# Pairs of chunks in the first expert matmul, state decay on GpSimd, and 64-column array tiles for PV and the state term, in a fused attention and MLP kernel

## The chip, the cores and the metric

The kernel runs on one core of one Trainium2 chip. The metric is device time in microseconds (us), the median of several executions. The time and the trace of a run are of the same single core. The calls ran on several chips, so runs of different calls are compared by their ratios to the kernel before, which ran beside them. All executions used here are in the undisturbed ("fast") state; the granted TensorE clock of the profiled ones is 0.996 to 1.000 of full.

## The reference

A chunked linear attention with decay feeds a two-layer MLP with an ELU between the layers. Cut to what matters:

```python
# B, H, S, D = 4, 8, 768, 64; x: 3072 tokens x 512; w_in 512 x 2048; w_out 2048 x 512
for b in range(nb):                       # blocks of 64 positions
    intra = einsum('bhic,bhjc->bhij', qb, kb) * Dmask
    intra = einsum('bhij,bhjd->bhid', intra, vb)            # "PV"
    inter = einsum('bhid,bhde->bhie', qb * lam_pow, kv_state)   # "state term"
    out[:, :, sl] = intra + inter
    kv_state = lam_block * kv_state + einsum('bhsd,bhse->bhde', kb * rev_pow, vb)
h = x @ w_in
g = where(h > 0, h, exp(min(h, 0)) - 1)
return g @ w_out
```

## The kernel before

The kernel works in chunks of 128 positions of one batch row: 24 chunks `g`, six per row. Each chunk goes through transposes of q and k (`T`, `psT`), scores (`S`, `psS`), a masked product (`E`, `pp`), PV with the state term (`P`, `psO`, copied to `xt`), and the state update (`U`, `psU`, `st`). The MLP takes `xt`: `mm1` makes 512 columns of h in one PSUM bank (`psH`), ScalarE (ACT) makes exp and relu of it, VectorE (DVE) combines them to `g`, and `mm2` accumulates the output in `psM`. TensorE (PE) runs a fixed list of these units. The opening is written out by hand (`OPEN`), the rest is generated from offsets (`AT`).

```python
GPE = 10                       # chunks below 10 are transposed on PE, the others by DMA
POOL_ORDER = "iota q1 k1 v1 v0 i1 i0 k2 q2 v2 o0 o1 i3 i2 ..."   # GpSimd: loads, k decay (d)
OPEN = "V0 Z1 z1 V1 ... T0 T1 S0 S1 P0 P1 1:0:0 T2 1:1:0 S2 2:0:0 ..."
# ... "1:g:j" is unit j of mm1 of chunk g, "2:g:j" of mm2
AT = {"W": -13, "T": -9, "S": -8, "P": -5, "U": -3}

def att_P(g):                                                  # PV and state term
    ...
    for hp in range(NHP):                                      # four pairs of heads
        for hh in range(2):
            b0 = 4 * hp + hh        # v stands beside zeros, so that 128 columns hold one head
            nc.tensor.matmul(po[:, hp, :], lhsT=vt[:, b0 : b0 + 2, :],          # L322
                rhs=Pt[(g, hh)][:, hp, :], start=(hh == 0), stop=(hh == 1 and cb == 0))
        if cb > 0:
            nc.tensor.matmul(po[:, hp, :], lhsT=st[b][cb % 2][:, hp, :],        # L327
                rhs=qt[:, hp, :], start=False, stop=True)
    ...

def att_U(g):                                                  # state update
    ...                                                        # four matmuls, psU
    for hh in range(2):
        ...
        (nc.gpsimd if g >= GPE else nc.vector).tensor_tensor(  # decay, L356
            out=tmp[r], in0=old[r, :, r], in1=upp[r]..., op=ALU.mult)
        nc.vector.tensor_tensor(out=new[r, :, r], in0=tmp[r], in1=pu[r, :, r], op=ALU.add)

def mm1(g, j):
    ...
    for f in range(FB):                                        # four blocks of 128 columns of h
        for kk in range(NHP):
            nc.tensor.matmul(pH[:, f, :], lhsT=wi16[i][:, kk, w * 128 : (w + 1) * 128],
                rhs=xt[g][:, kk, :], start=(kk == 0), stop=(kk == NHP - 1))     # L388
    nc.scalar.activation(e[:], pH[:], AF.Exp)
    nc.scalar.activation(pH[:], pH[:], AF.Relu)
```

## Time and profile before

| | before |
|---|---|
| time, median of 3 | 222.96 us (222.66 to 223.24) |
| span in the profile | 221.4 us |
| first matmul starts | 5.43 us |
| last matmul starts | 218.06 us |
| GpSimd busy | 88.6 us |
| VectorE busy | 138.6 us |

The lines of the page that the argument rests on stand in the prediction below. PE, DVE, ACT and POOL (GpSimd) are engines, PEld is weight loading on TensorE. A row of forty digits gives the busy tenths of forty equal slices. In the chain of work that ended last, each row is start, duration, engine, what was written and a count. A duration there runs until the next link takes over, so a stretch of PE links without a gap is PE's pace.

A busy PE is not a streaming PE, so I also took the start of every matmul from the trace and compared the distance to the next start with the distance seen in an undisturbed stream: 55.7 ns for 128 columns, 109 for 256, 215.7 for 512, and half of 55.7 where two tiles run at once. What is over is a **switch** where the two neighbours use different array tiles, and a **wait** otherwise (a switch over 0.3 us counts as 0.12 us of switch and the rest as wait). So PE's time from first to last start splits into stream, switches and waits. Before, these are 197.7 us, 3.0 us (26 switches) and 11.9 us. In the opening many matmuls of 128 columns start 107 ns apart, half the later rate, and this excess is counted under waits: some 2.9 us before, 2.5 after the change.

### The profile page before, as it was taken

How to read it: one execution, taken by the hardware profiler on the slowest of the kernel's cores; microseconds unless marked ns; L12 is line 12 of the kernel's file. 1: busy time of each engine (PE TensorE's matmuls, PEld its weight loads, DVE VectorE, ACT ScalarE, POOL GpSimd, SP SyncE). 2: the span in 40 equal slices, each digit the busy share in tenths (PEclk: the TensorE clock that was granted, in tenths of full speed). 3: DMA queues.
4: the chain of work that ended last, by engine and by line, in shares of the span. 5: the costliest groups of instructions: out<-in, count | busy, mean ns of one | idle time of the engine just before them, and what ended most of it. 6: DMA issues, size and time to landing. Idle time of an engine off the chain costs nothing.

```text
span 221.4 us, 6086 instructions
## 1 busy us (share of the span) xinstructions
PE 207.1 (94%) x2548; PEld 156.3 (71%) x2548; DVE 138.6 (63%) x238; ACT 134.8 (61%) x255; POOL 88.6 (40%) x102
## 2 busy tenths in 40 slices
PE   0598999999999999999999999999999999999993
PEld 0486677768768776787787787787787777777761
DVE  5744745489978978666666666656657646634330
ACT  5745657766768566636636636646646645656760
POOL 8996990829972809508508508122000000000000
PEclk9999999999999999999999999999999999999999
DMA  7999999999999999968998998803304401101102
GB/s 114 169 182 186 195 200 167 139 169 120 166 140 181 127 164 135 141 84 93 143 100 100 132 108 95 144 0 98 94 3 98 96 3 47 52 1 50 47 3 95
DMA packets 99804, 24.26 MB, mean 110 GB/s; under 512 B 90432, under 2 KB 96832, under 8 KB 99776
## 3 DMA queue, kind: packets, MB, share of 16 engines
q0 software_dynamic: 78720, 13.37, 83.8%
q1 hardware_dynamic: 20912, 10.49, 22.3%
q8 instruction: 20, 0.33, 0.6%
q14 instruction: 8, 0.07, 0.1%
q10 hardware_dynamic: 144, 0.00, 0.0%
HBM read 27.27 MB, written 6.29 MB: 152 GB/s over the span
## 4 chain that ended last, share of the span: by engine, by line
PE 79%; DVE 11%; ACT 5%; DMA 2%; issue 1%; SPq 0%; DVEq 0%; ACTq 0%
PE psH L388 34%; PE psM L409 33%; PE psO L322 5%; DVE g L376 3%; PE psS L300 3%; DVE stt L356 2%; DMA raw_k<-in_k_dram 2%; PE psO L327 2%; DVE pp L309 2%; PE psU L344 2%; DVE qT L288 1%; DVE st L360 1%; ACT e L393 1%; ACT psH L394 1%; PE psT L281 1%
## 5 line engine op out<-in xcount | busy, mean ns | idle before, releaser
L388 PEld LDWEIGHTS <-wi 128*128 128x128 f16 x1536 | 94.0, 98 | 22.0 <-issue 2.2
L388 PE MATMUL psH<-xt,wi 128*128 128x128 f16 x1536 | 102.2, 220 | 1.8 <-ACT xt L333 0.7
L393 ACT ACTIVATE e<-psH 128x512 f32<-128x512 f32 x96 | 57.3, 597 | 68.3 <-PE psH L388 68.0
L409 PE MATMUL psM<-wo,g 128*128 128x512 f16 (+1 forms) x388 | 97.6, 377 | 0.8 <-DVE osb L422 0.5
L376 DVE SCALAR_TENSOR_TENSOR g<-e,psH 128x512 f16<-128x512 f32 x96 | 65.6, 684 | 44.1 <-ACT psH L394 42.8
L394 ACT ACTIVATE psH<-psH 128x512 f32<-128x512 f32 x96 | 56.9, 593 | 0.0
L409 PEld LDWEIGHTS <-g 128*128 128x128 f16 x388 | 33.7, 98 | 26.8 <-issue 0.7
L309 DVE TENSOR_TENSOR pp<-psS,mask 128x512 f16<-128x512 f32 x48 | 30.7, 682 | 5.1 <-PE psS L300 5.1
L107 POOL DMA_DIRECT2D vz<-in_v_dram x14 | 15.1, 1085 | 38.5 <-PE psU L344 38.0
L169 POOL TENSOR_TENSOR kd<-kn,ks 128x512 f16<-128x512 f16 x20 | 21.3, 1073 | 11.2 <-DMA kn<-in_k_dram 10.6
L322 PE MATMUL psO<-pp,vz 128*128 128x128 f16 x192 | 19.1, 226 | 1.2 <-DVE pp L309 1.2
L360 DVE TENSOR_TENSOR st<-stt,psU 64x256 f16<-64x256 f32 x32 | 13.4, 419 | 7.3 <-PE psU L344 6.3
L335 DVE TENSOR_TENSOR xt<-psO,qs 128x512 f16<-128x512 f32 x14 | 9.7, 691 | 11.9 <-PE psO L327 11.9
L322 PEld LDWEIGHTS <-vz 128*128 128x128 f16 x192 | 15.1, 101 | 2.5 <-issue 1.8
L424 ACT COPY osb<-psM 128x512 f32<-128x512 f32 (+1 forms) x24 | 13.9, 579 | 4.5 <-PE psM L409 4.5
L356 POOL TENSOR_TENSOR stt<-st,upp 64x256 f32<-64x256 f16 x20 | 12.2, 608 | 10.3 <-DVE st L360 9.5
L107 POOL DMA_DIRECT2D qn<-in_q_dram x13 | 14.8, 1142 | 0.5 <-DMA wi<-in_moe_w_in_dram 0.3
L327 PE MATMUL psO<-qT,st 128*128 128x128 f16 x80 | 14.4, 219 | 0.0
L107 POOL DMA_DIRECT2D kn<-in_k_dram x13 | 14.4, 1107 | 0.0
L288 DVE TENSOR_TENSOR qT<-psT,qs 128x512 f16<-128x512 f16 x10 | 6.6, 681 | 5.2 <-PE psT L281 5.2
L281 PE MATMUL psT<-ident,qn 128*128 128x128 f16 x40 | 4.6, 247 | 5.4 <-DVE qn L122 5.4
L333 ACT CAST xt<-psO 128x512 f16<-128x512 f32 x10 | 5.9, 588 | 6.0 <-PE psO L322 4.0
(41 smaller groups left out, 90.2 us busy)
## 6 DMA issues: line engine op xcount, KB each, us to landing
out_dram<-osb SPq DMA_DIRECT2D x23, 256.0 KB, 3.4
qn<-in_q_dram POOLq DMA_DIRECT2D x10, 256.0 KB, 7.6
kn<-in_k_dram POOLq DMA_DIRECT2D x10, 256.0 KB, 7.4
vz<-in_v_dram POOLq DMA_DIRECT2D x10, 256.0 KB, 8.2
wi<-in_moe_w_in_dram POOLq DMA_DIRECT2D x8, 256.0 KB, 8.3
wo<-in_moe_w_out_dram POOLq DMA_DIRECT2D x8, 256.0 KB, 8.8
vz<-in_v_dram POOLq DMA_DIRECT2D x4, 128.0 KB, 5.9
qn<-in_q_dram POOLq DMA_DIRECT2D x3, 128.0 KB, 6.4
```

Source lines behind the costliest of these rows:

```text
L107: nc.gpsimd.dma_start(out=dst.rearrange("p b h d -> p (b h) d"), in_=src)
L169: nc.gpsimd.tensor_tensor(out=kd[:], in0=of(kg, g), in1=ks[:].unsqueeze(2).broadcast_to([128, H, 64]), op=ALU.mult,)
L309: nc.vector.tensor_tensor(out=P[:], in0=pts[hh][:], in1=mask[:, hh::2, :], op=ALU.mult)
L322: nc.tensor.matmul(po[:, hp, :], lhsT=vt[:, b0 : b0 + 2, :], rhs=Pt[(g, hh)][:, hp, :], start=(hh == 0), stop=(hh == 1 and cb == 0), skip_ ...
L327: nc.tensor.matmul(po[:, hp, :], lhsT=st[b][cb % 2][:, hp, :], rhs=qt[:, hp, :], start=False, stop=True, skip_group_check=True,)
L356: (nc.gpsimd if g >= GPE else nc.vector).tensor_tensor(out=tmp[r], in0=old[r, :, r], in1=upp[r].unsqueeze(2).broadcast_to([64, NHP, 64]), ...
L360: nc.vector.tensor_tensor(out=new[r, :, r], in0=tmp[r], in1=pu[r, :, r], op=ALU.add)
L376: nc.vector.scalar_tensor_tensor(out=g[:], in0=e[:], scalar=-1.0, in1=r[:], op0=ALU.add, op1=ALU.min)
L388: nc.tensor.matmul(pH[:, f, :], lhsT=wi16[i][:, kk, w * 128 : (w + 1) * 128], rhs=xt[g][:, kk, :], start=(kk == 0), stop=(kk == NHP - 1),)
L393: nc.scalar.activation(e[:], pH[:], AF.Exp)
L394: nc.scalar.activation(pH[:], pH[:], AF.Relu)
L409: nc.tensor.matmul(psM[g][:, cols], lhsT=gts[(g, j)][:, f, :], rhs=wo16[i][:, w, cols], start=first and f == 0, stop=end and f == FB - 1, ...
```

## The change

Four things are meant to take work off TensorE and VectorE:

- `mm1` takes two chunks at once from chunk 4 on: one weight load and 256 moving columns.
- PV and the state term stop multiplying by zeros: each head gets its own 64-column half of the array, and two heads run at the same time.
- The state decay goes to GpSimd for all chunks, as its own step (`att_M`) ahead of the update.
- Chunks 8 and 9 are transposed by DMA (`GPE = 8`), and order of loads and units is rearranged to suit, with seven units of mm2 held back for the end (`LAGU = 7`).

```diff
-    GPE = 10
+    GPE = 8
+    GSIZE = {**{g: 1 for g in range(4)}, **{g: 2 for g in range(4, NG, 2)}}
     POOL_ORDER = (
-        "iota q1 k1 v1 v0 i1 i0 k2 q2 v2 o0 o1 i3 i2 q3 i5 k3 o2 d0 o3 i4 v3 o5 o4 d2 o7 i6 d3 "
+        "k2 v1 q2 iota q1 k1 i1 v0 i0 o1 v2 i3 o0 i2 q3 o2 k3 d0 d2 i4 d1 i5 o3 o7 v3 o5 o4 d3 "
...
     OPEN = (
-        "V0 Z1 z1 V1 z0 v3:1 Z0 z3 z2 T0 T1 S0 S1 P0 P1 1:0:0 T2 1:1:0 S2 2:0:0 Z2 P2 1:2:0 "
+        "v3:1 Z2 Z0 z2 Z1 V0 z0 T0 z3 z1 V1 T1 S0 T2 S1 P0 S2 P1 1:0:0 P2 U0 1:1:0 1:2:0 2:0:0 "
...
-    LAGU, LAG_END = 3, 4
+    LAGU = 7
...
-    nc.scalar.dma_start(out=lam_b[:], in_=lam.unsqueeze(0).broadcast_to([128, H]))
+    nc.sync.dma_start(out=lam_b[:], in_=lam.unsqueeze(0).broadcast_to([128, H]))
...     # raw_q stays on the sync queue, behind lam_b; raw_k goes to ScalarE's queue
         for hp in range(NHP):
-            for hh in range(2):
-                b0 = 4 * hp + hh
+            for hh, r in enumerate(R):                  # R: partitions 0-63 and 64-127
                 nc.tensor.matmul(
-                    po[:, hp, :], lhsT=vt[:, b0 : b0 + 2, :], rhs=Pt[(g, hh)][:, hp, :],
+                    po[r, hp, :], lhsT=vt[:, 4 * hp + 2 * hh, :], rhs=Pt[(g, hh)][:, hp, :],
...
             if cb > 0:
-                nc.tensor.matmul(
-                    po[:, hp, :], lhsT=st[b][cb % 2][:, hp, :], rhs=qt[:, hp, :],
+                for r in R:
+                    nc.tensor.matmul(
+                        po[r, hp, :], lhsT=st[b][cb % 2][:, hp, r], rhs=qt[:, hp, :],
...
+    def att_M(g):                                       # the decay, always GpSimd
...
-        for f in range(FB):
-            i, w = wi_of[j * FB + f]
+        for f in range(FB // n):                        # n: 1 or 2 chunks
+            i, w = wi_of[j * (FB // n) + f]
             for kk in range(NHP):
                 nc.tensor.matmul(
-                    pH[:, f, :], lhsT=wi16[i][:, kk, w * 128 : (w + 1) * 128],
-                    rhs=xt[g][:, kk, :], start=(kk == 0), stop=(kk == NHP - 1),
+                    pH[:, f * n * 128 : (f + 1) * n * 128],
+                    lhsT=wi16[i][:, kk, w * 128 : (w + 1) * 128],
+                    rhs=xg[g0][:, kk, :], start=(kk == 0), stop=(kk == NHP - 1),
                 )
```

In the changed kernel's trace the lines are: mm1 L428 (was L388), mm2 L450 (L409), PV L332 (L322), state term L338 (L327), scores L310 (L300), update L382 (L344), decay L365 (L356), `st` L393 (L360), `g` L411 (L376), transposes L291 (L281).

## The prediction

> **What bounds the kernel now.** I read the page's busy shares and 40 slices first, then the chain that ended last in order of time, then the waits of 20 to 90 us.
>
> ```profile
> PE 207.1 (94%) x2548; PEld 156.3 (71%) x2548; DVE 138.6 (63%) x238; ACT 134.8 (61%) x255; POOL 88.6 (40%) x102
> ...
> PE   0598999999999999999999999999999999999993
> ...
> DMA  7999999999999999968998998803304401101102
> ```
>
> TensorE (PE) is busy in every slice but the ends, at the full clock. The DMA engines are full until about 95 us, VectorE (DVE) never. Busy does not mean streaming, so I take the pace from the chain:
>
> ```profile
> 102.98 0.45 PE psH L388 x8
> 103.43 0.55 PE psS L300 x16
> 103.98 0.97 PE psM L409 x4
> 104.95 0.89 PE psH L388 x16
> 105.84 0.86 PE psM L409 x4
> ...
> 109.36 0.11 PE psO L322 x2
> 109.47 0.06 PE psO L327
> ```
>
> Sixteen mm1 matmuls of 128 columns take 0.89 us, 56 ns each; four mm2 matmuls of 512 columns take 0.86 us, 216 ns each. PV and the state term (psO) also go at 56 ns. Nothing lies between them: in this stretch PE runs at its streaming rate, so mm1's many weight loads are hidden already. Multiplying out the page's counts: mm1 1536 x 55.7 ns = 85.6 us; mm2 380 x 216 plus 8 of 256 columns x 109 = 82.8; PV 192 x 55.7 = 10.7; state term 80 and state update 80, 4.5 each; transposes 80, 4.5; scores 192 in row-tile pairs, 5.4. Sum 197.9 us. The first matmul starts at 5.4 us and the last at 218.1. Start to start, the trace holds 14.9 us beyond the nominal rates: 8.7 before 20 us, 3.8 from 20 to 90, 1.3 from 90 to 200, 1.1 afterwards. That, and the stream, is all that the change can take away.
>
> The scores are the one tiled step now (64 rows by 128 columns), so they are my yardstick for the new tiles. Their 16 should stream as 8 pairs in 8 x 55.7 = 0.45 us. They hold the chain for 0.55, and the mm2 behind them shows 0.97 where 0.86 is usual: about 0.21 us per group goes on entering and leaving the tiled mode, some 0.1 each way. The 1.3 us lost between 90 and 200 is these switches.
>
> **What the Trainium skill says.**
> - "TensorE: Matmul & The Clock Gate", Back-to-back issue gap, gives about 81 ns per matmul of 128 columns in a stream with weight loads, and N/2.4 + 2.5 ns for the isolated gap. This trace has 56 ns in the full stream: the second form holds, the 81 does not. So doubling the moving columns can't bring the 81 to 55 that it suggests.
> - "TensorEngine Tiling (Array Packing)", Key Properties: changing the tiling mode drains the engine. The trace agrees (0.21 us per group of scores).
> - The same page, Restrictions: column tiling disables Fast Weight Load. Nothing in this trace has a 64-column weight load; this is the main unknown.
> - "GPSIMD Engine Reference", Engine selection: two-input elementwise work is about twice as slow on GpSimd. For this small op the trace does not agree, as the next rows show.
>
> ```profile
> L356 POOL TENSOR_TENSOR stt<-st,upp 64x256 f32<-64x256 f16 x20 | 12.2, 608 | 10.3 <-DVE st L360 9.5
> ...
> L356 DVE TENSOR_TENSOR stt<-st,upp 64x256 f32<-64x256 f16 x12 | 8.0, 666 | 0.1
> ```
>
> **The change part by part.** The order of the built program gives counts: mm1 becomes 256 matmuls of 128 columns (chunks 0 to 3) and 640 of 256; PV 192 and state term 160, all with 64 output rows; 64 transposes instead of 80; mm2, scores and state update as before.
>
> 1. mm1 in pairs. 640 x 2 x 55.7 = 71.3 us becomes 640 x 109 = 69.8 (the 256-column mm2 matmuls start 109 ns apart). Gain 1.5 us. Halving 1280 weight loads gains nothing on PE, since they are hidden.
> 2. PV and state term. Before: a late chunk's 12 matmuls x 55.7 = 0.67 us, standing between full-array work. After: 16 half-width matmuls, as 8 concurrent pairs x 55.7 = 0.45, plus the two switches of 0.19 to 0.21: 0.64 to 0.66. Gain 0.02 each for 20 chunks; for the four first chunks 8 x 55.7 = 0.45 against 4 x 55.7 + 0.2 = 0.42. Halving the stream saves 5.3 us and the switches take nearly all of it back: net 0.5 to 0.8 us gained.
> 3. Chunks 8 and 9 go to DMA transposes: 16 x 55.7 = 0.9 us off PE. The transposes take 2.4 to 8.9 us to land (median 4.5), so they must be issued early; the new order puts them several units ahead of their use.
> 4. State decay to GpSimd in the opening: 12 x 0.67 = 8 us off VectorE, 12 x 0.61 = 7.3 on GpSimd (88.6 us busy of 221). PE's stalls there are short. Of the 2.4 us lost between 40 and 90, three groups of scores explain 0.6. A freer VectorE and the new order may take 1 to 1.5 of the remaining 1.8.
> 5. New opening. Three loads now precede the iota, so the identity, the exponentials and the first transpose come about 1.2 us later; GpSimd issues a load in 0.9 to 1.1 us. Against that, chunk 2's scores and PV fill the wait for the first weights. I walked the order at the measured pace of landings (0.9 us for a single chunk, 1.3 for a weight slab, 1.7 for a pair): mm1's second chunk-0 unit comes 1 us earlier than now, but the transposes of chunks 4 and 5 need the loads behind all sixteen slabs, landing at 38 and 39.7 us now. The bytes ahead of them are the same, so that lead is mostly given back. I book 0, with -1 to +1.
> 6. The end. Seven mm2 units (0.86 us each) are now held back for the end instead of four. It can remove the 0.36 us stall at 201 us; the last matmuls, the copy and the store stay. Gain 0.3.
>
> Sum: 1.5 + 0.65 + 0.9 + 1.2 + 0 + 0.3 = 4.5 us, from 222.96 to about 218.4; I state 218.2.
>
> **The rivals.**
> - The column tiles load slowly. The skill's LDWEIGHTS section gives P/1.2 ns, an estimated 53 ns for 64 columns. If both halves load at once, that hides under 55.7 ns and part 2 stands. If they take turns, a pair costs 107 ns: 176 pairs x 51 = 9 us, and the kernel would be at 227. For it: no such load in this trace. Against: the scores' two row tiles start 4 ns apart, loads included. I give it 15%.
> - GpSimd becomes the feeder that waits. It is in order, and its decay products now stand between loads. Before, it already sat 38 us for psU ahead of vz loads, without a PE stall; but a decay behind a late state would delay loads while the queues are full, so PE could wait for DMA at chunks 4 to 9: +1 to +3 us, near 221.
> - The opening pays more than I book. 8.7 of the 14.9 us lie before 20 us; if landings are not the limit, 2 to 3 us more come off, near 215.5. For it: the new order starts PE work on three chunks before mm1. Against: the DMA slices are full from 4 us.
> - mm1 was limited by weight loads after all, and halving them gives some 15 us. PEld's 71% speaks for it; the chain's 56 ns rules it out.
>
> **Range and chances.** 218.5 us is the 2% line and my sum lies on it. The terms 1, 3 and 6 are sure within a few tenths; 4 and 5 move by 1 to 3 us together; the first rival adds 9. So 214.5 to 223. Faster by over 2%: 0.52, since the sure terms are small but the whole opening was evidently rearranged to make them pay; within 2%: 0.39; slower: 0.09, nearly all of it the first rival.
>
> **What would show it.** Start to start, the new mm1 matmuls should stand 109 ns apart and those of psO in pairs 56 ns apart, with about 0.1 us on either side; 107 ns between pairs would be the first rival. A late chunk's psO should hold the chain for about 0.65 us. VectorE should lose some 8 us, PE busy some 4, and GpSimd gain 7. Between 20 and 90 us the loss beyond nominal, without switches, should fall from about 3 to 1.5 us. If PE waits for kn, qn or qT, the second rival holds. The prediction is wrong if the psO pairs don't overlap, if the switches cost much more or less than the scores' 0.21 us, or if the opening gains or loses over 2 us.

## The result, and the profile after

The changed kernel takes **221.28 us** (220.76 to 221.56, 4 runs) against 222.81 us for the kernel before in the same rounds. The ratio is 0.9927, with a 95% interval of 0.9901 to 0.9954. A ratio is the mean time of one kernel's fast runs over that of the other's of the same rounds, so it isn't quite the ratio of the medians. That is 0.7% faster: inside the 2% that counts as the same, inside the stated range, and a third of the 2.1% (222.96 to 218.2 us) that was forecast.

The page of the changed kernel, the same rows as before:

```profile
PE 204.3 (93%) x1972; PEld 139.1 (63%) x1972; DVE 130.8 (60%) x226; ACT 132.4 (60%) x251; POOL 95.5 (43%) x114
...
PE   0398999999999998999999999999999999999993
...
DMA  5999999999999999979909919114114110111021
```

VectorE lost 7.8 us and GpSimd gained 6.9, as worked out. PE's busy time fell by 2.8 us only. The second PE slice shows 3 where it showed 5: PE starts later. The DMA engines are full in the opening as before.

The chain that ended last, in the steady part:

```profile
104.45 0.87 PE psH L428 x8
105.33 0.18 PE psO L332 x2
105.50 0.06 PE psO L338 x2
105.56 0.06 PE psO L332 x2
...
105.84 0.06 PE psO L338 x2
105.89 0.97 PE psM L450 x4
106.86 0.87 PE psH L428 x8
```

Each 0.06 us link now holds two half-width matmuls, so the tiles do run at once and the first rival (loads that take turns) is ruled out. But the first link holds 0.18 us, and the mm2 behind shows 0.97 where 0.86 is usual. PV with the state term of one chunk holds the chain from 105.33 to 105.89, and 0.11 us more: 0.67 us. Before, twelve full matmuls also took 0.67 us, from 109.36 in the chain that the prediction quotes to 110.03:

```profile
109.97 0.06 PE psO L327
110.03 0.86 PE psM L409 x4
```

The third that the tiles take off the stream (0.67 to 0.45 us) went into entering and leaving them.

The decay in the list of groups; the columns are busy us and the mean ns of one:

```profile
L365 POOL TENSOR_TENSOR stt<-st,upp 64x256 f32<-64x256 f16 x32 | 19.5, 610 | 1.4
```

All 32 are on GpSimd, at 610 ns each.

The start-to-start split of both kernels, in us:

| part of PE's time | before | after | change |
|---|---|---|---|
| start of the first matmul | 5.43 | 7.25 | +1.82 |
| waits before 20 us | 8.23 | 6.21 | -2.02 |
| waits 20 to 90 us | 2.47 | 2.98 | +0.51 |
| waits after 90 us | 1.22 | 0.93 | -0.29 |
| switches | 3.01 (26) | 8.82 (73) | +5.81 |
| stream | 197.69 | 189.92 | -7.77 |
| last matmul's start to the end of the span | 3.3 | 3.6 | +0.2 |
| span | 221.4 | 219.7 | -1.7 |

So the stream fell by what was worked out (1.5 for mm1, 5.3 for the tiles, 0.9 for the transposes). Switches took 5.8 us of it back, and the waits and the start together gave nothing. Each column is one profiled execution: in a second one of the changed kernel (the control below) the waits are 5.22 us before 20 us and 3.54 from 20 to 90, so single rows, and the span, are good to about 1 us.

### The profile page after: what moved, and what is told of

It is laid out like the page before. It is cut to its first block, busy times and chain, and to the rows that moved or that the text cites. A ratio compares the mean times of both kernels' runs of the same rounds, so it can differ in the third digit from the quotient of the medians.

```text
span 219.7 us, 4953 instructions
## 1 busy us (share of the span) xinstructions
PE 204.3 (93%) x1972; PEld 139.1 (63%) x1972; DVE 130.8 (60%) x226; ACT 132.4 (60%) x251; POOL 95.5 (43%) x114
## 4 chain that ended last, share of the span: by engine, by line
PE 88%; DVE 3%; DMA 2%; POOL 2%; ACT 2%; issue 1%; POOLq 0%; DVEq 0%; ACTq 0%
PE psM L450 39%; PE psH L428 37%; PE psO L332 4%; PE psS L310 3%; DMA kn<-in_k_dram 2%; PE psU L382 2%; PE psO L338 2%; DVE pp L319 1%; PE psT L291 1%; DVE st L391 1%; POOL qn L110 1%; DVE g L411 1%; DVE qT L298 1%; ACT e L434 1%; POOL kn L110 0%
## 5 line engine op out<-in xcount | busy, mean ns | idle before, releaser
L428 PE MATMUL psH<-xt,wi 128*128 128x256 f16 (+1 forms) x896 | 100.4, 259 | 2.2 <-DVE g L411 1.8
L450 PE MATMUL psM<-wo,g 128*128 128x512 f16 (+1 forms) x388 | 97.2, 378 | 0.5 <-DVE osb L463 0.5
L411 DVE SCALAR_TENSOR_TENSOR g<-e,psH 128x512 f16<-128x512 f32 x96 | 65.9, 686 | 49.7 <-ACT psH L435 48.8
L428 PEld LDWEIGHTS <-wi 128*128 128x128 f16 x896 | 77.7, 99 | 27.6 <-DVE g L411 3.2
L450 PEld LDWEIGHTS <-g 128*128 128x128 f16 x388 | 35.1, 98 | 29.0 <-issue 0.7
L365 POOL TENSOR_TENSOR stt<-st,upp 64x256 f32<-64x256 f16 x32 | 19.5, 610 | 1.4
L393 DVE TENSOR_TENSOR st<-stt,psU 64x256 f16<-64x256 f32 x32 | 13.4, 418 | 7.6 <-PE psU L382 6.9
L352 DVE TENSOR_TENSOR xt<-psO,qs 128x512 f16<-128x512 f32 x16 | 11.1, 691 | 11.0 <-PE psO L338 11.0
L332 PE MATMUL psO<-pp,vz 128*64 128x128 f16 x192 | 14.2, 236 | 0.3 <-DVE pp L319 0.3
L332 PEld LDWEIGHTS <-vz 128*64 128x64 f16 x192 | 10.0, 115 | 5.8 <-issue 5.5
L291 PE MATMUL psT<-ident,qn 128*128 128x128 f16 x32 | 3.8, 253 | 8.6 <-DVE qn L128 7.2
L338 PE MATMUL psO<-qT,st 128*64 128x128 f16 x160 | 11.2, 219 | 0.0
L338 PEld LDWEIGHTS <-st 128*64 128x64 f16 x160 | 9.0, 110 | 0.0
L310 PE MATMUL psS<-qT,kT 64*128 64x128 f16 x192 | 8.6, 229 | 0.1
```

Source lines behind the costliest of these rows:

```text
L310: nc.tensor.matmul(psS[g][hh][:, hp, :], lhsT=kt[r, hp, :], rhs=qt[r, hp, :], start=True, stop=True,)
L332: nc.tensor.matmul(po[r, hp, :], lhsT=vt[:, 4 * hp + 2 * hh, :], rhs=Pt[(g, hh)][:, hp, :], start=True, stop=(cb == 0), skip_group_check=True,
L338: nc.tensor.matmul(po[r, hp, :], lhsT=st[b][cb % 2][:, hp, r], rhs=qt[:, hp, :], start=False, stop=True, skip_group_check=True,)
L365: nc.gpsimd.tensor_tensor(out=tmp[r], in0=old[r, :, r], in1=upp[r].unsqueeze(2).broadcast_to([64, NHP, 64]), op=ALU.mult,)
L411: nc.vector.scalar_tensor_tensor(out=g[:].rearrange("p f c t -> p (f c t)"), in0=e[:], scalar=-1.0, in1=r[:], op0=ALU.add, op1=ALU.min,)
L428: nc.tensor.matmul(pH[:, f * n * 128 : (f + 1) * n * 128], lhsT=wi16[i][:, kk, w * 128 : (w + 1) * 128], rhs=xg[g0][:, kk, :], start=(kk = ...
```

## The experiments

The theory after the result: (a) the column tiles gain nothing, because switching the array costs what they save; (b) pairing mm1 is worth its 1.5 us and no more; (c) the waits of 20 to 90 us did not shrink because of the new order, not because of VectorE's load; (d) the opening is set by loads. The rivals are that the tiles pay and the loss is elsewhere, that weight loads mattered, and that a busier GpSimd or DMA is the new limit. Each run was timed in five rounds beside the kernel before, whose median was 222.83 to 223.08 us. The control is the changed kernel run again with the last group:

> The changed kernel again, unaltered, as the control for the other runs of this call: 220.8 to 221.6 us, as first measured. Its runs should scatter by up to 1 us, because TensorE leaves half rate at 12 us in some executions and at 16 to 18 us in others.

It took 221.24 us, 220.46 to 221.55 in six runs (ratio 0.9917, interval 0.9894 to 0.9940). Its profiled execution spans 218.8 us against 219.7 in the first one, with the same instructions: its matmuls of 128 columns, tiled pairs included, stop starting 107 ns apart, half the later rate, at 13.4 us instead of 18.2 (a row of full-array ones ends at 12.3, which is what the text above goes by). Differences under half a microsecond are therefore read from the trace, and the times only have to agree.

### PV back on the full array

```diff
-                    po[r, hp, :], lhsT=vt[:, 4 * hp + 2 * hh, :], rhs=Pt[(g, hh)][:, hp, :],
+                    po[:, hp, :], lhsT=vt[:, b0 : b0 + 2, :], rhs=Pt[(g, hh)][:, hp, :],
...
+    # and the state term as one matmul of 128 columns
```

> The changed kernel with PV and the state term back on the full array (12 matmuls of 128 columns instead of 16 half-width ones); all else as changed. Theory: entering and leaving the column tiles costs as much as they save, since the trace of the changed kernel has 47 more mode switches, 5.8 us, for 5.3 us less stream. So 0.0 to 0.6 us faster than the changed kernel, about 220.9 us, with 26 switches and PE stream up by 5.3 us. Rival: the tiles do pay and the expected gain was lost elsewhere; then this run is 3 to 5 us slower, 224 to 226.

Measured: 220.92 us, ratio 0.9903 (0.9885 to 0.9920). The stream rose to 195.3 us (+5.35) and the switches fell to 28, 3.6 us (-5.2). The waits before 90 us were within 0.7 us in total. The chain of this run:

```profile
103.95 0.87 PE psH L428 x8
104.83 0.11 PE psO L333 x2
...
105.44 0.06 PE psO L338
105.50 0.86 PE psM L450 x4
```

PV holds 104.83 to 105.50, again 0.67 us, and the mm2 behind it has its plain 0.86. The rival (3 to 5 us slower) falls. The run is 0.3 to 0.5 us faster than the changed kernel in the medians and means; the intervals overlap, so only "no gain from the tiles" is shown.

### The tiles alone, in the kernel before

```diff
 # kernel before, att_P alone
-                    po[:, hp, :], lhsT=vt[:, b0 : b0 + 2, :], rhs=Pt[(g, hh)][:, hp, :],
+                    po[r, hp, :], lhsT=vt[:, 4 * hp + 2 * hh, :], rhs=Pt[(g, hh)][:, hp, :],
...
```

> The kernel before with only PV and the state term put in column tiles (352 half-width matmuls instead of 272 full ones), order and all else as before. Theory: stream down by 5.3 us, some 46 more mode switches at 0.11 to 0.12 us, 5.0 to 5.5 us, so within 0.5 us of before (222.3 to 223.3). Rival: tiles pay (218 to 219); other rival: tile loads take turns (over 226).

Measured: 223.16 us against 223.08, ratio 0.9994 (0.9976 to 1.0012). The stream is 5.3 us shorter than in the kernel before (192.4 against 197.7). The switches are 71 against 26 and cost 8.1 us against 3.0. The same exchange of 5.3 for 5.1 us holds in the old order, with nothing else changed: (a) is shown from both sides.

### The PV of both chunks of a pair side by side

```diff
-            (f"P{g}", AT["P"]), (f"P{g + 1}", AT["P"] + 1),
+            (f"P{g}", AT["P"]), (f"P{g + 1}", AT["P"]),
```

> The changed kernel with the PV of both chunks of a pair put back to back in the part after the opening (chunks 10 to 23, 7 pairs), so that each pair enters and leaves the column tiles once. Theory of the switches: two fewer per pair at 0.11 us, 14 in all, 1.5 us faster than the changed kernel, about 219.8 us, with 59 switches in the trace. Rival: the cost is per change of output half or per first matmul of a chunk, not per mode switch: no gain (within 0.4 us). A third way: the second chunk's softmax-free product (pp) is not ready yet and PE waits for VectorE: slower.

Measured: 219.88 us, ratio 0.9858 (0.9840 to 0.9877), 1.4 us faster than the changed kernel. The trace has 59 switches, 7.3 us (1.5 less), with the same stream. The chain of this run:

```profile
105.10 0.18 PE psO L332 x2
105.28 0.06 PE psO L338 x2
...
106.06 0.06 PE psO L338 x2
106.11 0.97 PE psM L450 x4
```

Two chunks hold 105.10 to 106.11 and 0.11 us of the mm2 behind: 1.12 us, where two separate ones take 1.34. The cost is paid per entry into the tiled mode: 32 half-width matmuls pay what 16 pay. This is the direct measure of the switch: 14 fewer, 1.5 us.

### mm1 in 128 columns again, in the new order

```diff
-                    pH[:, f * n * 128 : (f + 1) * n * 128],
-                    rhs=xg[g0][:, kk, :],
+                        pH[:, (f * n + c) * 128 : (f * n + c + 1) * 128],     # c: 0 and 1
+                        rhs=xg[g0][:, kk, c * 128 : (c + 1) * 128],
```

> The changed kernel with each 256-column matmul of mm1 split into two of 128 columns with a weight load each, in the same order. Theory: weight loads are hidden, the pair gains only 2 x 55.7 - 109 = 2.4 ns on each of 640, so 1.5 us slower than the changed kernel, about 222.8 us. Rival 1: halving the weight loads is worth more (PEld was 71% busy): 4 us slower or more. Rival 2: PE is not what ends last, and nothing changes (within 0.4 us).

Measured: 223.01 us, ratio 1.0003 (0.9993 to 1.0014): 1.7 us slower than the changed kernel, and all that the change had gained. The stream is 191.5 us, 1.5 more, with switches and waits unchanged to 0.3 us. So (b) holds: 640 further weight loads cost nothing beyond 2.4 ns per pair of matmuls.

### The decay on VectorE again

```diff
     def att_M(g, eng=None):
+        if eng is None and g < 10:
+            return
...
     # att_U, just ahead of the add:
+        if B <= g < 10:
+            att_M(g, nc.vector)
```

> The changed kernel with the state decay of chunks 4 to 9 on VectorE again, at the update, as before. The prediction's step 4 says that the 8 us taken off VectorE remove 1 to 1.5 us of PE waits between 20 and 90 us: then this run is 1 us or more slower than the changed kernel, over 222.2. New theory: VectorE's load was not what PE waited for, the waits of 20 to 90 us did not shrink (2.5 before, 3.0 after), and this run is within 0.4 us of the changed kernel.

Measured: 223.14 us, ratio 1.0000 (0.9985 to 1.0015). My new theory (c) fell, and the prediction's mechanism holds: this run is 1.9 us slower than the changed kernel, and its waits of 20 to 90 us are 6.0 us against 3.0 (3.5 in the control). Most of it is one place. The chain of this run:

```profile
63.90 0.69 DVE g L415
64.59 0.34 DVE stt L367
...
65.83 0.42 DVE st L397
...
68.06 0.70 DVE g L415
...
68.81 1.05 PE psH L432 x8
```

The updates of chunks 7 and 6 stand close together in the new order. With the decay, eight operations (`stt` and `st`) come between two `g`, and mm1 waits 1.9 us for a free `psH` bank. Without the decay the same place waits 0.2 us. So the decay's move is worth 1.9 us here. That the new order had already spent it, by packing the updates where VectorE had no room before, is an inference. Whether it would gain in the old order was not run, since GpSimd's list there has all loads ahead of the decay.

### Two waits that the new order makes itself

The first place is at 50.9 us. The timeline of the changed kernel (start, duration, engine and instruction; in brackets the idle time and what ended it):

```profile
50.70 0.40 PE L382 MATMUL psU<-vz,kd 128*128 128x128 f16 x4
51.44 1.03 PE L428 MATMUL psH<-xt,wi 128*128 128x256 f16 x8 [0.35 <-ACT xt L350]
```

A pair's first mm1 unit needs both chunks' `xt`, and here it stands right behind the second chunk's PV.

```diff
-... P5 U5 1:4:1 2:3:3 ...
+... P5 U5 2:3:3 1:4:1 ...
```

> The changed kernel with one token moved: mm2 unit 2:3:3 ahead of the first mm1 unit of pair 4 and 5 (1:4:1), which waits for the second chunk's xt. Theory: the pairing itself makes that wait of 0.51 us at 50.9 us (the unit needs both chunks' PV), and a unit of other work in front fills it: 0.3 to 0.5 us faster than the changed kernel (220.8 to 221.0). Rival: the wait only moves, to the next wait for g near 56 us: no change.

Measured: 220.46 us, ratio 0.9889 (0.9862 to 0.9916). The 0.51 us wait is gone from the trace, while the next one (at 53.2 us) is 0.58 instead of 0.50. The total of 40 to 60 us fell by 0.37. The time fell by 0.8 us, but the six runs lie in two groups (220.1 to 220.6 and 221.3), and the profiled run is one in which TensorE reached full rate at 14 us instead of 18. About 0.4 us is the wait's; the rest is not explained by it, and the interval overlaps the control's.

The second place is at 85 us. Changed kernel:

```profile
83.78 0.62 PE L310 MATMUL psS<-qT,kT 64*128 64x128 f16 x16
84.34 1.05 PE L428 MATMUL psH<-xt,wi 128*128 128x256 f16 x8
86.16 1.05 PE L428 MATMUL psH<-xt,wi 128*128 128x256 f16 x8 [0.77 <-DVE g L411]
```

Behind the scores two mm1 units follow each other, because the rule that holds seven mm2 units back skips one there. VectorE first has `pp` to make, so `g` is late. From start to start the second unit loses 0.94 us. The kernel before lost 0.61 us at the same place, although an mm2 unit stood between: there a decay held VectorE ahead of `g` (timeline of the kernel before):

```profile
83.77 0.86 DVE L356 TENSOR_TENSOR stt<-st,upp 64x256 f32<-64x256 f16 x1
...
85.86 0.84 PE L388 MATMUL psH<-xt,wi 128*128 128x128 f16 x12 [0.45 <-DVE g L376]
```

The run puts the mm2 unit back between the two:

```diff
-    LAGU = 7
+    LAGU = 6
```

> The changed kernel with six mm2 units held back for the end instead of seven (one number). In the changed order the scores of chunks 10 and 11 are followed by two mm1 units in a row, and the second waits 0.94 us for g at 85 us; with six held back an mm2 unit stands between them. Theory: the wait is the order's own, not VectorE's load: 0.5 to 0.9 us faster than the control, with the wait at 85 us gone and the end as before (six units, 5.2 us, still cover the 2.1 us from mm1 to g). Rival: VectorE is behind there anyway and the wait moves to the next unit: within 0.3 us.

Measured: 220.29 us, ratio 0.9881 (0.9859 to 0.9902), 0.95 us faster than the control. The same place:

```profile
84.41 1.05 PE L428 MATMUL psH<-xt,wi 128*128 128x256 f16 x8
85.30 1.03 PE L450 MATMUL psM<-wo,g 128*128 128x512 f16 x4
86.23 1.05 PE L428 MATMUL psH<-xt,wi 128*128 128x256 f16 x8
```

The wait is gone and did not move. The waits of 60 to 90 us fell from 1.25 to 0.39 us, and the end stayed at 0.69.

### The opening

```diff
-        "k2 v1 q2 iota q1 k1 i1 v0 i0 o1 ...
+        "iota q1 k1 k2 v1 q2 i1 v0 i0 o1 ...
```

> The changed kernel with the iota and the loads of q1 and k1 put ahead of k2, v1 and q2 again, as before; all else as changed. Theory: the late first transposes (7.25 us against 5.43) and the wait for q1 and k1 (landing at 9.6 and 10.5 us) shift the whole stream, since PE hardly waits between 20 and 50 us in the changed kernel; first transpose at 5.5 to 6.8 us and 0.8 to 1.8 us faster than the changed kernel, 219.5 to 220.5. Rival, as the prediction had it: the loads behind all sixteen weight slabs set the pace of the opening, so an earlier start is given back; within 0.4 us of the changed kernel, with a new wait for kn or qn near 40 us.

Measured: 220.49 us, ratio 0.9891 (0.9871 to 0.9912), 0.6 to 0.8 us faster than the changed kernel, at the edge of the theory; its interval overlaps the control's (0.9894 to 0.9940). The start moved only to 7.00 us, because `raw_q` now sets it. The next run moves that too:

```diff
 # on top of the load order
-    nc.sync.dma_start(out=lam_b[:], ...)            # raw_k on nc.scalar
+    nc.scalar.dma_start(out=lam_b[:], ...)          # raw_q, raw_k on nc.sync
```

> e4_load_order with the lambda row on ScalarE's queue and both raw loads, q first, on SyncE's, as in the kernel before. Theory: raw_q lands at about 4.9 us instead of 6.2 and the first transpose starts near 5.5 us instead of 7.0. If the raw loads set the opening, 0.5 to 1.3 us faster than e4_load_order (219.2 to 220.0). Rival: from there the loads of chunk 1 and 2 set the pace and it is given back, within 0.3 us of e4_load_order (220.2 to 220.8).

Measured: 220.64 us, ratio 0.9890 (0.9865 to 0.9915), the same as with the load order alone. The first transpose starts at 5.47 us, 1.5 us earlier, and all of it is given back. Waits before 20 us rise from 5.26 to 6.60 us. The timeline of this run shows where the lead goes:

```profile
9.30 0.61 PE L310 MATMUL psS<-qT,kT 64*128 64x128 f16 x8 [1.05 <-ACT kT L299]
...
23.41 0.40 PE L291 MATMUL psT<-ident,kn 128*128 128x128 f16 x4 [0.40 <-DMA kn<-in_k_dram]
```

With the load order alone the first scores start at 9.22 us, so the whole lead is gone there. They wait for `kT` of the first chunk, which ScalarE makes behind its cast of `raw_k` (at 6.12 us here, at 5.71 with the load order alone) and seven other small operations. Some 0.2 us of lead appears again by 12.3 us, and at 23.4 us both runs stand level, waiting for chunk 3's k. So (d) is half right. Getting chunk 1's q and k sooner goes with some 0.7 us. A still earlier start is worth nothing, first because of ScalarE's list and only then because of loads. Whether a shorter list on ScalarE would keep the lead was not run.

### The end

```diff
-            if end:
-                out_of(g, cols, nc.vector if last and hi == 0 else nc.scalar)
+            # last tile: both halves' matmuls first, then both copies
```

> The changed kernel with both halves of the last output tile computed before either is copied out. Theory: the last 256-column group waits 0.68 us for VectorE's copy out of the same PSUM tile, in both kernels, which is a fixed share of the end that neither the change nor its prediction touched; 0.4 to 0.6 us faster than the control. Rival: the two copies from one bank take turns, and only 0.2 us is left.

Measured: 221.09 us, ratio 0.9918, against 221.24 and 0.9917 for the control: nothing. The 0.68 us wait is gone, but the chain shows why it isn't gained:

```profile
215.23 0.44 DVE osb L466
215.66 0.02 issue
215.69 0.37 ACT osb L468
```

ScalarE's copy starts only when VectorE's has ended, so the copies take turns; whether the program's order or the chip makes them do so was not tested. The end was and stays the same in both kernels.

### Together

The kernel with the load order, adjacent PV in the opening and after it, full-array PV for chunks 0 to 3, six units held back, mm2 work ahead of the first unit of pair 4 and 5, and the new end:

```diff
-... P4 E5 V3 2:3:1 U4 2:3:2 P5 U5 1:4:1 2:3:3 U3 ...
+... E5 V3 2:3:1 2:3:2 P4 P5 U4 U5 2:3:3 U3 1:4:1 ...
-... P6 1:4:6 U7 P7 U6 ...
+... 1:4:6 P6 P7 U7 U6 ...
-... P8 1:6:5 1:6:6 2:6:1 P9 U9 ...
+... 1:6:5 1:6:6 2:6:1 P8 P9 U9 ...
```

> All that the experiments point to: the changed kernel with the load order of e4, the PV of both chunks of a pair adjacent in the opening too (chunks 4 to 23, 10 pairs, 20 switches fewer), full-array PV for chunks 0 to 3, six units held back, mm2 work ahead of the first mm1 unit of pair 4 and 5, and the end of e8. If the gains add: 0.8 + 2.2 + 0.2 + 0.7 + 0.4 + 0.5 = 4.8 us under the control, about 216.3 us; since the early ones are partly given back to the loads, 216.3 to 218. Rival: adjacent PV in the opening makes PE wait for pp or xt and it is no better than e5_pv_adjacent (219.9).

Measured: **218.56 us**, ratio 0.9809 (0.9785 to 0.9833): 2.7 us under the control, 4.5 under the kernel before. It beats both kernels; at 1.9% with an interval across the 2% line, whether it is faster by 2% stays unclear. The switches fell to 48 and 5.5 us, with the stream at 190.8. It misses the 216.3 to 218 that was expected. The end's 0.5 us was never there, the load order's gain is partly given back, and PE has new waits of 0.44 and 0.86 us for VectorE's `g`: near 62 us behind two `pp`, near 67 us behind four `st` operations of two chunks.

All timed runs (median us, ratio to the kernel before, then start-to-start in us of the profiled run):

| run | median | ratio | stream | switches | waits |
|---|---|---|---|---|---|
| kernel before | 222.81 | 1 | 197.7 | 3.0 (26) | 11.9 |
| changed kernel | 221.28 | 0.9927 | 189.9 | 8.8 (73) | 10.1 |
| control, again | 221.24 | 0.9917 | 189.9 | 8.4 (73) | 9.7 |
| PV on the full array | 220.92 | 0.9903 | 195.3 | 3.6 (28) | 9.5 |
| tiles alone in before | 223.16 | 0.9994 | 192.4 | 8.1 (71) | 12.0 |
| PV of a pair adjacent | 219.88 | 0.9858 | 189.9 | 7.3 (59) | 10.1 |
| mm1 in 128 columns | 223.01 | 1.0003 | 191.5 | 8.8 (73) | 9.9 |
| decay on VectorE | 223.14 | 1.0000 | 189.9 | 8.4 (73) | 12.2 |
| mm2 unit ahead | 220.46 | 0.9889 | 189.9 | 8.6 (73) | 9.0 |
| six held back | 220.29 | 0.9881 | 189.9 | 8.8 (73) | 9.3 |
| load order | 220.49 | 0.9891 | 189.9 | 8.5 (73) | 9.7 |
| load order and queues | 220.64 | 0.9890 | 189.9 | 8.4 (73) | 11.3 |
| new end | 221.09 | 0.9918 | 189.9 | 8.6 (73) | 9.1 |
| together | 218.56 | 0.9809 | 190.8 | 5.5 (48) | 9.7 |

## Why the prediction was right or wrong

The sum of the steps was 4.5 us; the profile's span fell by 1.7 and the time by 1.5. By its own steps:

1. **mm1 in pairs, 1.5 us: right.** The trace's stream and the run that undid it give 1.5 and 1.7 us, and the rival of 15 us from fewer weight loads is excluded.
2. **PV and state term, 0.5 to 0.8 us gained: wrong in the size of one term.** The mechanism was right: tiles overlap, 5.3 us less stream, a switch at either side. The step put the two switches of a late chunk at 0.19 to 0.21 us from the scores. Measured, a late chunk takes 0.67 us in either form, so they cost 0.22 us. And the step booked 0.2 us for each first chunk, too little for the opening, where the matmuls still run at half rate and each single switch costs 0.19 to 0.24 us. The tiles' own switches, from the run with PV back on the full array, are 45 and cost 5.2 us, where the step's figures allow some 4.8. So the step gave 0.1 to 0.3 us of PE's time rather than 0.65; the time of the tiles alone, in the old order, says 0.1 us with an uncertainty of 0.4. The other 0.6 us by which the switches rose, by this split, stand at the scores in the new opening.
3. **Transposes, 0.9 us: as predicted in the stream** (64 instead of 80). It was not run alone.
4. **VectorE's relief, 1 to 1.5 us: the step that failed most.** It read the waits of 20 to 90 us as something that the old order would keep and a freer VectorE would shorten. They rose by 0.5 us instead (by 1.1 in the control). The relief is real (1.9 us slower without it). But the new order makes waits of its own: 0.51 us for the second chunk's `xt`, and 0.94 us for two mm1 units in a row where the old order lost 0.61, each shown by a run that removes it. Two readings under the step were off as well. Between 40 and 90 us stand four groups of scores, not three, so 1.5 us of waits were there to remove, not 1.8. And VectorE's mean of 666 ns for a decay mixes six of 407 to 423 ns with six of 657 to 1279 ns, all while GpSimd was at work; the short ones beat GpSimd's 602 to 612. The step counted a saving on an engine without walking the new order past it.
5. **The opening, 0 with -1 to +1: right in size, in part by luck.** PE starts 1.8 us later, more than the 1.2 that the step gave. The load order is not all of it: the late `raw_q`, behind the lambda row on SyncE's queue, holds the start at 7.00 us in the run with the old load order, and the step had not counted that. The start and the waits before 20 us together changed by -0.2 us, by -1.2 in the control. That a lead is given back is shown by the run with the queues restored, but ScalarE's list took it first, not the loads. And the 8.7 us before 20 us held some 2.9 us of half rate, which the page's full granted clock hid from the prediction.
6. **The end, 0.3 us: right for the wait at 201 us**, which is gone.

Of the rivals, slow tile loads and limiting weight loads are excluded. GpSimd as the new feeder did not show: PE waited for no late pair of loads between 40 and 90 us. The forecast of "faster by over 2%" at 0.52 failed because step 4 was 1.7 us too high and step 2 some 0.5, and because the scores' switches in the new opening, which no step counted, took 0.6 us; with these as measured, the sum is 1.7 us.

## What to carry to other kernels

Array tiles for small matmuls pay by the length of the run inside them: here about 0.22 us to enter and leave, so eight pairs of 128 columns break even and sixteen in one go save a sixth. Put tiled work side by side before tiling more of it. When an engine that isn't the bound is relieved, walk the new order unit by unit to see which wait it ends; here the order that came with it made new ones. And look at single durations before comparing two engines by a mean.

## What the Trainium skill lacked or had wrong

- "TensorE: Matmul & The Clock Gate", Back-to-back issue gap: it has a sustained 81 ns per matmul of 128 columns and 131 ns for 512 with weight loads. Here streams with a weight load for each matmul run at 55.7 and 215.7 ns, and 109 ns for 256; the page's isolated formula is the one that holds.
- "TensorEngine Tiling (Array Packing)", Key Properties: it says that a change of mode drains the engine, without a size. Here a chunk of PV pays 0.22 us for entering and leaving column tiles at full rate, and about twice that in the opening at half rate.
- The same page, Restrictions: it says that column tiling disables Fast Weight Load. In these runs no cost of that is visible with 128 moving columns: pairs of half-width matmuls, each with its own load, start 52 to 53 ns after the second of the pair before, 3 ns apart within a pair. Only the gap behind the first pair is longer, about 75 ns.
- The same page, Theoretical Speedup, has "up to 2x" for a dimension of 64. Here 352 half-width matmuls, 16 in a chunk (8 in the first four), saved 5.3 us of stream and gained nothing in the time (ratio 0.9994, 0.9976 to 1.0012), since each chunk pays the switches.
- "GPSIMD Engine Reference", Engine selection: two-input work about twice as slow as on VectorE. In the kernel before the 64 x 256 decay takes 602 to 612 ns on GpSimd. On VectorE six of twelve take 407 to 423 ns, so GpSimd is about 1.5 times as slow, and the other six 657 to 1279 ns, all while GpSimd is at work, four of them beside its k decay (`kd`).
- "TensorE: Matmul & The Clock Gate", Part 1, has matmuls of 128 columns 107 ns apart while the array is cold, and the change to full rate about 4 us into sustained activity. Here the 107 ns last until 13.4 us in one execution of the changed kernel and 18.2 in another, with the first matmul at 7.25 us and pauses between, and the granted clock reads 1.00 between 12 and 18 us. The page says that the start varies from run to run, but has no number for one broken by such pauses. Whether this is what scatters the runs by up to 1 us is not shown.
